# A 128-byte tile that nobody uses, placed ahead of the activation tiles in SBUF

## The chip, the cores and the metric

The kernel runs on one core of one Trainium2 chip. The metric is the device time of one execution in microseconds (us), taken as the median of several runs. All inputs start in HBM and the output ends there.

## The reference

The computation is a block-local attention followed by a feed-forward layer with a squared ReLU. Only what matters is shown:

```python
# q, k, v: (8, 8, 576, 64) float32; w_in: (512, 2048), w_out: (2048, 512) float64
q_c, k_c, v_c = (t.reshape(B, H, S // 64, 64, D) for t in (q, k, v))
scores = np.matmul(q_c, k_c.transpose(0, 1, 2, 4, 3)) / np.sqrt(D)
attn = softmax(scores)                       # over each chunk of 64 keys
x = np.matmul(attn, v_c)                     # back to (4608 tokens, 512)
h = x @ w_in
g = np.maximum(h, 0.0) ** 2
out = g @ w_out                              # (4608, 512) float32
```

## The kernel before

**Tiling.** The 4608 tokens are 36 "pairs" of two 64-token chunks, 128 tokens each, and the pairs are gathered into nine blocks of four (512 tokens). A block's attention output is kept transposed in SBUF as two tiles, `xh` (the value rounded to the matmul's reduced float type) and `xl` (the remainder), made by `x_of`; there are two buffers of each, and block b uses buffer b % 2. The hidden dimension of 2048 is cut into 16 slices of 128.

**Feed-forward.** For each block and slice a `Step` does twelve 128x512 products into `h` (`mm_in`, L514): the stationary operand is a 128x128 piece of the weights `wi`, the moving operand is 512 columns of `xh` or `xl`, and each of the four pieces of the contraction takes three products (high by high, high by low, low by high). ScalarE takes the ReLU of `h` into `g` (L525), VectorE, or ScalarE in the first two blocks, squares it (L529, L531), and the square is split into `gh` (ScalarE, L538) and `gl` (VectorE, L541). Two slices later twelve products go into the four accumulators `o` (`mm_out`, L551): here pieces of `gh` or `gl` are stationary and 512 columns of `wo` move. That is 9 x 16 x 24 = 3456 products in all. After a block's last slice the accumulators are copied to `ob` (L565) and stored.

**Attention.** The first eight pairs go through the class `Pair`, in the opening of the kernel and beside the conversion of the weights. The other 28 go through `Quad`: every so often three small groups of products (L321, L331, L291) are put between two products of the feed-forward.

**Weights.** They come as 64-bit floats. For each of 32 items a DMA brings the raw words, and ScalarE and VectorE turn them into high and low parts in seven steps (L147 to L186), with a working tile from the pool `wst`.

**Order of work.** A `Plan` lists all operations with assumed costs, and a small list scheduler writes out each engine's instructions in a fixed order. It looks at costs, dependences and ranks; addresses in SBUF are no part of it.

**Places in SBUF.** The pools are opened one after the other and lie in that order in each partition: `const` (identity, the raw and converted weights, and the leading pairs' q and k under the same tags), `att` (four small tiles of 32 bytes, L427 to L447 and their like in `Quad`), `xp` (`xh`, `xl`, and in the end the last block's output under the same tag), `gp` (`g`, `gh`, `gl`, `ob`), `raw` (q and k as loaded), `wst`, and then the pools `nat` or `late` of the attention. In the built program of before, `const` tiles of the weights begin at byte 17,056 of the partition, `att` at 148,128, the first `xh` at 148,256 and `g` at 181,024. Weight tiles are 4096 bytes apart, the buffers of x 8192, those of g 2048, so that all large tiles of `const` begin 160 bytes past a multiple of 256, and all large tiles behind `att` 32 bytes past one. Of the leading pairs' value tiles `vbd` (L475), the first two lie in `nat` and the next two in `const`.

Of the kernel before, what the change touches and what calls it, by code (L numbers as in the profile page):

```python
# [10 lines left out]
F32 = mybir.dt.float32  # L11
# [9 lines left out]
def kernel(  # L21
# [24 lines left out]
    P = 128  # L46
# [28 lines left out]
    att = ctx.enter_context(tc.tile_pool(name="att", bufs=1))  # L75
# [4 lines left out]
        x: ctx.enter_context(tc.tile_pool(name=f"ps_{x}", bufs=1, space=bass.MemoryType.PSUM))  # L80
        for x in ("o", "h", "at")
    }
    turn_at = itertools.count()

    both = psum["at"].tile([P, 2, DM], F32, name="both", tag="both")
# [931 lines left out]
```

## Time and profile before

| | |
|---|---|
| median of 3 runs | 911.04 us (909.97 to 911.22) |
| the profiled execution's own time | 911.28 us |
| its span, first to last instruction | 909.5 us |
| mean granted TensorE clock | 0.997 |
| instructions | 14995 |

The profile names engines PE (TensorE's matmuls), PEld (its weight loads, which overlap the matmuls), DVE (VectorE), ACT (ScalarE), POOL (GpSimd) and SP (SyncE, which issues most DMAs). A group of instructions is named by its line in the kernel and by out<-in with the program's tile names. A window's row gives, for each engine, the busy time in that stretch and in brackets the number of instructions. The chain of waits follows the work that ended last back from the last instruction; each of its pieces has a start, a length in us and a name, with the number of instructions in it. "Issue" there is time in which an engine waited for nothing that the profile shows.

### The profile page before, as it was taken

What the parts mean: (1) busy time and instruction counts of PE and PEld (TensorE: products, weight loads), DVE (VectorE), ACT (ScalarE), POOL (GpSimd) and SP (SyncE); (2) the same over time, 40 slices, a digit from 0 to 9 for tenths busy, and PEclk for the clock granted to TensorE, in tenths of its full rate; (3) what the DMA queues carried; (4) which work ended last, traced back from release to release, by engine and by line L of the source; (5) the groups of instructions that cost most, each with busy time, mean ns of one, the idle gap of its engine ahead of it and who ended that gap; (6) DMA issues with size and microseconds to landing.
All of it is one profiled execution on the core that took longest, in us unless ns stands there. A gap on an engine that the chain in (4) does not pass through costs nothing.

```text
span 909.5 us, 14995 instructions
## 1 busy us (share of the span) xinstructions
PE 897.6 (99%) x6046; PEld 724.9 (80%) x6046; DVE 427.1 (47%) x746; ACT 329.9 (36%) x565; POOL 6.1 (1%) x12
## 2 busy tenths in 40 slices
PE   8899999999999999999999999999999999999998
PEld 7677777888888888888888888888888888878886
DVE  5999992333444445444443343444444443223222
ACT  4798873334322223222322222223222322222221
POOL 2000000000000000000000000000000000000000
PEclk9999999999999999999999999999999999999999
DMA  9876533222222223111311131123222210001001
GB/s 196 261 210 177 168 65 97 36 48 46 70 48 36 35 35 83 32 33 31 79 33 32 33 81 29 33 35 81 36 36 36 51 42 1 1 1 47 1 1 46
DMA packets 193237, 55.52 MB, mean 61 GB/s; under 512 B 178192, under 2 KB 186640, under 8 KB 193168
## 3 DMA queue, kind: packets, MB, share of 16 engines
q1 hardware_dynamic: 190912, 53.91, 25.7%
q8 instruction: 47, 0.77, 0.4%
q10 hardware_dynamic: 2256, 0.66, 0.3%
q14 instruction: 22, 0.18, 0.1%
HBM read 45.09 MB, written 9.44 MB: 60 GB/s over the span
## 4 chain that ended last, share of the span: by engine, by line
PE 90%; DVE 5%; ACT 3%; issue 1%; POOL 0%; POOLq 0%; ACTq 0%; DVEq 0%
PE h L514 41%; PE o L551 41%; PE both L331 2%; PE both L291 1%; PE pt L321 1%; DVE gl L541 1%; PE both L741 1%; DVE wia L172 0%; ACT qbd L413 0%; DVE wi L186 0%; DVE wia L165 0%; DVE woa L165 0%; PE sc L425 0%; ACT wi L177 0%; DVE woa L172 0%
## 5 line engine op out<-in xcount | busy, mean ns | idle before, releaser
L514 PE MATMUL h<-xh,wi 128*128 128x512 f32 x1152 | 393.4, 398 | 0.1
L551 PE MATMUL o<-wo,gh 128*128 128x512 f32 x1152 | 361.7, 395 | 0.4 <-ACT ob L565 0.4
L514 PEld LDWEIGHTS h<-xh,wi 128*128 128x128 f32 x1152 | 216.1, 188 | 52.2 <-DVE wi L186 0.5
L551 PEld LDWEIGHTS o<-wo,gh 128*128 128x128 f32 x1152 | 215.8, 188 | 50.8 <-ACT ob L565 0.9
L551 PE MATMUL o<-wo,gl 128*128 128x512 f32 x576 | 227.0, 394 | 0.0
L514 PE MATMUL h<-xl,wi 128*128 128x512 f32 x576 | 226.0, 393 | 0.0
L541 DVE TENSOR_TENSOR gl<-g,gh 128x512 fp32r<-128x512 f32 x144 | 99.3, 690 | 207.3 <-ACT gh L538 204.2
L538 ACT CAST gh<-g 128x512 fp32r<-128x512 f32 x144 | 89.4, 621 | 225.7 <-PE o L551 188.4
L525 ACT ACTIVATE g<-h 128x512 f32<-128x512 f32 x144 | 85.6, 594 | 228.8 <-PE h L514 226.5
L529 DVE TENSOR_TENSOR g<-g 128x512 f32<-128x512 f32 x112 | 76.4, 682 | 184.9 <-ACT g L525 184.9
L551 PEld LDWEIGHTS o<-wo,gl 128*128 128x128 f32 x576 | 108.1, 188 | 25.7
L514 PEld LDWEIGHTS h<-xl,wi 128*128 128x128 f32 x576 | 108.5, 188 | 24.0
L297 DVE TENSOR_REDUCE m<-both 128x8 f32<-128x512 f32 x28 | 19.3, 691 | 55.9 <-ACT xh L341 51.8
L307 ACT ACTIVATE e<-e 128x512 f32<-128x512 f32 x28 | 17.7, 632 | 49.6 <-DVE e L301 49.6
L327 ACT COPY p<-pt 128x512 f32<-128x512 f32 x28 | 16.4, 585 | 20.4 <-PE pt L321 20.4
L341 ACT CAST xh<-both 128x512 fp32r<-128x512 f32 x28 | 16.4, 587 | 14.4 <-PE both L291 13.4
L531 ACT ACTIVATE g<-g 128x512 f32<-128x512 f32 x32 | 20.3, 635 | 0.6
L343 DVE TENSOR_TENSOR xl<-both,xh 128x512 fp32r<-128x512 f32 x28 | 19.1, 681 | 2.1 <-ACT xh L341 2.1
L277 DVE STREAM_TRANSPOSE qt<-q_raw 128x512 f32<-128x512 f32 x28 | 19.6, 700 | 0.0
L331 PEld LDWEIGHTS both<-p,v_raw 64*64 64x64 f32 x896 | 15.6, 134 | 4.9 <-issue 4.9
L331 PE MATMUL both<-p,v_raw 64*64 64x64 f32 x896 | 19.4, 224 | 0.0
L316 DVE TENSOR_TENSOR e<-e,z 128x512 f32<-128x512 f32 x28 | 19.2, 685 | 0.1
(85 smaller groups left out, 461.6 us busy)
## 6 DMA issues: line engine op xcount, KB each, us to landing
wiraw<-in_moe_w_in_dram SPq DMA_DIRECT2D x16, 512.0 KB, 6.6
woraw<-in_moe_w_out_dram SPq DMA_DIRECT2D x16, 512.0 KB, 5.8
out_dram<-ob SPq DMA_DIRECT2D x32, 256.0 KB, 2.0
q_raw<-in_q_dram SPq DMA_DIRECT2D x224, 32.0 KB, 2.2
k_raw<-in_k_dram SPq DMA_DIRECT2D x224, 32.0 KB, 2.2
v_raw<-in_v_dram SPq DMA_DIRECT2D x56, 128.0 KB, 3.3
vbd<-in_v_dram SPq DMA_DIRECT2D x32, 64.0 KB, 3.3
qk_raw<-in_q_dram SPq DMA_DIRECT2D x14, 128.0 KB, 4.8
```

The lines of the kernel that those rows point to most:

```text
L277: nc.vector.transpose(t.rearrange("p h i -> p (h i)"), pairs[self.pair][nm].rearrange("p h a d -> p (h a d)"))
L297: nc.vector.tensor_reduce(self.m, four[:, :, 0], axis=AX.X, op=ALU.max)
L316: nc.vector.tensor_tensor(self.e, self.e, self.z.broadcast_to([P, HH, 2, CH]), op=ALU.mult)
L331: nc.tensor.matmul(four[to, c, 1, h2], self.v[own, 2 * h2 + w], self.p[own, h2, w], start=True, stop=True)
L343: nc.vector.tensor_tensor(xl, four[:, :, 1], xh.bitcast(F32), op=ALU.subtract)
L514: nc.tensor.matmul(self.h[:, :self.n], a[:, c], bb[:, c, :self.n], start=c == 0 and i == 0, stop=last,)
L525: nc.scalar.activation(self.g, self.h[:, :self.n], AF.Relu)
L529: nc.vector.tensor_tensor(self.g, self.g, self.g, op=ALU.mult)
L531: nc.scalar.activation(self.g, self.g, AF.Square)
L538: nc.scalar.copy(self.gh[:, :self.n], self.g)
L541: nc.vector.tensor_tensor(self.gl[:, :self.n], self.g, self.gh.bitcast(F32)[:, :self.n], op=ALU.subtract)
L551: nc.tensor.matmul(acc[b, j], a[:, j * P:(j + 1) * P], bb, start=f == 0 and i == 0, stop=f == NF - 1 and i == 2,)
```

## The change

One tile of 128 partitions by 32 float32 values, 128 bytes in each partition, is taken from the pool `att` ahead of everything else in it. Nothing writes it and nothing reads it.

```diff
--- before.py
+++ after.py
@@ -80,6 +80,7 @@
         x: ctx.enter_context(tc.tile_pool(name=f"ps_{x}", bufs=1, space=bass.MemoryType.PSUM))
         for x in ("o", "h", "at")
     }
+    att.tile([P, 32], F32, name="edge")
     turn_at = itertools.count()
 
     both = psum["at"].tile([P, 2, DM], F32, name="both", tag="both")
```

The instructions of all five engines, and their order, are the same in both built programs (2757 rows of PE in the merged listing, 747 of DVE, 564 of ACT, 17 of POOL, 175 of SP). What differs is the place in SBUF of everything behind `const`: the small tiles of `att`, `xh`, `xl`, `g`, `gh`, `gl`, `ob`, `raw`, `wst`, `nat` and `late` all lie 128 bytes higher, the first `xh` at 148,384. The tiles of `const` and everything in PSUM stay where they were. The moved large tiles thus begin 160 bytes past a multiple of 256, as the weights do and did. The last tile ends 128 bytes later, at byte 228,256 of the partition.

## The prediction

> **What bounds the kernel now.** I read the page first, then the chain of waits, the windows by stage, and last the groups by line.
>
> ```profile
> span 909.5 us, 14995 instructions
> PE 897.6 (99%) x6046; PEld 724.9 (80%) x6046; DVE 427.1 (47%) x746; ACT 329.9 (36%) x565; POOL 6.1 (1%) x12
> PE 90%; DVE 5%; ACT 3%; issue 1%; POOL 0%; POOLq 0%; ACTq 0%; DVEq 0%
> ```
>
> PE is busy in 99% of the span, and it holds 90% of the chain that ended last. So TensorE sets the time in nine tenths of the chain; where the other tenth lies, the windows show (busy us, and instructions in brackets):
>
> ```profile
> core 0: us, PE busy (x) PEld busy (x) DVE busy (x) ACT busy (x) POOL busy (x), PEclk, DMA share, GB/s
> 0.00:33.00 33.00, 27.90 (x380) 23.44 (x381) 23.21 (x45) 17.90 (x32) 6.05 (x12) 0.95 0.93 230
> 33.00:117.00 84.00, 81.45 (x584) 63.43 (x582) 81.00 (x160) 73.21 (x133) 0.00 (x0) 1.00 0.67 192
> 230.00:806.00 576.00, 576.00 (x3935) 467.81 (x3936) 243.89 (x410) 165.17 (x277) 0.00 (x0) 1.00 0.20 41
> ```
>
> In the first 117 us VectorE is the full engine (81.00 of 84 us between 33 and 117): the weights are converted there and PE waits for it. From 230 to 806 us PE is never idle, and DVE and ACT work less than half the time. A change that adds no instruction can therefore act in three ways only: the pace of a product in the PE stage, the length of a vector or scalar instruction in the opening, or the landing of a transfer that somebody waits for. The pace comes from the chain, which merges the twelve products of a group (start us, length us):
>
> ```profile
> 521.23 2.78 PE o L551 x12
> 524.01 2.78 PE h L514 x12
> 537.93 2.78 PE o L551 x12
> 540.71 0.69 PE h L514 x3
> 810.55 2.80 PE h L514 x12
> 813.35 2.80 PE o L551 x12
> 897.25 8.42 PE o L551 x36
> ```
>
> From 521.23 to 540.71 there are seven groups in 19.48 us, 2.783 us each or 231.9 ns a product. From 810.55 to 897.25 there are 31 groups in 86.70 us, 2.797 us each or 233.1 ns a product. So there are two paces, 0.014 us a group apart, and each holds for long stretches with `h` and `o` alike; between them lies an insertion of attention products or a wait. I take the pace for a rhythm into which PE falls after a disturbance. What picks it the trace does not tell, and that matters for a rival below.
>
> **The change part by part.**
>
> *The tile itself.* It has no writer and no reader: no instruction, no wait, no transfer. The five instruction streams are the same in both programs, so no queue is passed and no wait is added. Cost: 0.
>
> *The products of the feed-forward.* In `h` a stationary weight piece (160 past a multiple of 256) meets a moving piece of x (now 32 past, then 160). In `o` it is the other way round: g is stationary and moved, `wo` moves through PE and keeps its place. If the distance between the two operands within 256 bytes set the pace, it would change from 128 to 0 for all 3456 products. The trace of before has one place where the same instruction stands at both distances: the values of the leading pairs, L475, where `vbd` of pairs 0 and 1 lies behind `att`, like the other operand `tt`, and that of pairs 2 and 3 in `const`. Pair 0, at distance 0, and pair 3, at distance 128:
>
> ```profile
> 17.99 1.15 PE L475 MATMUL both<-tt,vbd 128*64 128x64 f32 x32
> 31.34 1.15 PE L475 MATMUL xt<-tt,vbd 128*64 128x64 f32 x32
> ```
>
> Both take 1.15 us for 32. That is a narrower product (64 columns, not 512), so it bounds rather than proves: one step of the printed 0.01 us in 1.15 is 0.9%. The second bound is the pair of paces above. If all went at 2.783, the groups that ran at 2.797 would gain; if all went at 2.797, the long middle would lose. The counts per stretch, from the windows of L514 and of L551 in that order:
>
> ```profile
> 117.00:183.00 66.00, 32.78 (x134) 24.68 (x133) 1.00 0.28 58
> 196.00:230.00 34.00, 15.91 (x63) 11.74 (x63) 1.00 0.28 48
> 230.00:806.00 576.00, 289.85 (x1155) 215.18 (x1156) 1.00 0.20 41
> 806.00:906.00 100.00, 49.08 (x200) 37.12 (x198) 1.00 0.04 14
> ...
> 117.00:183.00 66.00, 33.34 (x132) 24.54 (x132) 1.00 0.28 58
> 196.00:230.00 34.00, 17.83 (x72) 13.44 (x72) 1.00 0.28 48
> 230.00:806.00 576.00, 282.72 (x1152) 216.63 (x1152) 1.00 0.20 41
> 806.00:906.00 100.00, 55.88 (x228) 42.79 (x228) 1.00 0.04 14
> ```
>
> Slow stretches: (134 + 132 + 63 + 72 + 200 + 228) / 12 = 69 groups, worth 69 x 0.014 = 1.0 us. Fast stretch: (1155 + 1152) / 12 = 192 groups, worth 192 x 0.014 = 2.7 us. So the term lies between -1.0 and +2.7 us. I take 0, since L475, the row where the distance alone differs, shows nothing.
>
> [...]
>
> *Vector and scalar instructions of the opening.* These are the instructions that fill 81.00 us of DVE between 33 and 117. Some mix a tile of `const` with a moved one, some use moved tiles alone:
>
> ```profile
> L541 DVE TENSOR_TENSOR gl<-g,gh 128x512 fp32r<-128x512 f32 x144 | 99.3, 690 | 207.3 <-ACT gh L538 204.2
> L529 DVE TENSOR_TENSOR g<-g 128x512 f32<-128x512 f32 x112 | 76.4, 682 | 184.9 <-ACT g L525 184.9
> L186 DVE TENSOR_TENSOR wi<-wia,wi 128x512 fp32r<-128x512 f32 x16 | 10.9, 684 | 1.2 <-ACT wi L177 1.0
> L165 DVE SCALAR_TENSOR_TENSOR wia<-wiraw,wia 128x512 uint32<-128x512 uint32 x16 | 10.9, 683 | 0.1
> L186 DVE TENSOR_TENSOR wo<-woa,wo 128x512 fp32r<-128x512 f32 x16 | 10.8, 676 | 0.4 <-ACT wo L177 0.4
> L538 ACT CAST gh<-g 128x512 fp32r<-128x512 f32 x144 | 89.4, 621 | 225.7 <-PE o L551 188.4 <-DVE g L529 37.3
> L177 ACT CAST wi<-wia 128x512 fp32r<-128x512 f32 x16 | 9.9, 619 | 4.9 <-DVE wia L172 4.8
> ```
>
> `gl` and the square read and write moved tiles alone (690 and 682 ns); L186 and L165 mix the two sides (676 to 684 ns). The casts of ScalarE are 621 ns within the moved tiles and 619 ns from a moved tile into `const`. Mixed or not, the vector rows lie between 676 and 690 ns, 1% to either side of their middle, and the larger value belongs to instructions that start after a wait. On 81.00 us of DVE, 1% is 0.8 us; so this term lies between -0.8 and +0.8 us, and I take 0.
>
> *Transfers.* What the opening waits for goes into `const` (the weights' words, and the leading pairs' q and k) and stays in place; of what it waits for only `vbd` of pairs 0 and 1 is moved. In the stretch from 230 to 806 us PE is never idle, so nothing that lands there is waited for. The end is the one place where a transfer from a moved tile is bare: the last half of the last store, issued by ACT.
>
> ```profile
> out_dram<-ob_last SPq DMA_DIRECT2D x1, 128.0 KB, 2.0
> out_dram<-ob_last ACTq DMA_DIRECT2D x1, 128.0 KB, 2.1
> ```
>
> The two halves of the last tile's store, equal in size, land in 2.0 and 2.1 us, so 0.1 us to either side is what I allow, and take 0. [...]
>
> **The sum.** Profiled execution 911.28 us (its span of 909.5 and 1.8 around it) + 0 + 0 + 0 + 0 = 911.28 us. The median of before is 0.24 us below its profiled execution, so in medians the forecast is **911.0 us**. The three runs of before spread from 909.97 to 911.22, that is 0.14%; a difference under 0.2% (1.8 us) is about what a measurement of this kernel cannot tell from none.
>
> **The rivals.**
>
> *Slower: the middle falls into the slow rhythm.* If the rhythm depends on where the operands lie, or on how the first products after an insertion meet, the 192 groups between 230 and 806 us may run at 2.797 us as the last 31 do. For it: both paces occur in one execution of one program, so something slight decides. Against: through that whole stretch every insertion was followed by the fast pace, and x alternates there between two buffers 16,384 bytes apart. Price 2.7 us, time 911.0 + 2.7 = 913.7 us. It counts as slower from 1.8 / 0.014 = 129 groups on, two thirds of the middle. Chance 0.12.
>
> *Faster: the distance of 128 costs something now.* If products slow down when their operands lie 128 apart within 256 bytes, the change takes the cost away in all 3456. For it: two paces exist, so a product of 512 columns can be quicker than another. Against: L475, and the vector rows, which make no difference between mixed and unmixed. Priced with the one step that the trace shows, 0.014 us in each of the 288 groups, it is 4.0 us, and the time 907.0 us; it counts as faster from 1.8 / 288 = 6 ns a group on, half a nanosecond a product. The slow stretches turning fast alone are 1.0 us and stay inside the band. Chance 0.08.
>
> *The change does not do what it says.* A tile without a reader could have been left out of the layout. But the built program has x at 148,384 and not 148,256, so it is moved; had it not been, the forecast would be the same 911.0 us. No chance of its own.
>
> **How the numbers follow.** The forecast, nothing that can be measured, has the remaining 0.80. The low end is the forecast with all slow groups turned fast and a run as far below its median as the lowest of before was: 911.04 - 0.97 - 1.07 = 909.0 us. That also holds the vector term's -0.8. The high end is the slower rival with a run as far above: 913.7 + 0.2 = 913.9 us. What is left out is the faster rival. Chances: faster by over 0.2% is 0.08, within 0.2% is 0.80, slower by over 0.2% is 0.12. The likeliest case by itself is 909.2 to 912.8 us.
>
> **What would show it.** In the profile after: groups of twelve at 2.783 us between 230 and 806 us and at 2.797 at the end; the vector rows between 676 and 690 ns; 81 us of DVE between 33 and 117; the last store in 2.0 to 2.1 us. If the middle shows 2.80, the slower rival is right. If a third pace appears, or L551 and L514 part from each other, the place of the operands matters in a way that L475 did not show. If the opening ends at another time than 117 us with the same paces behind it, the cause is in the vector stage or in a transfer.

## The result and the profile after

The changed kernel takes 895.03 us (894.47 to 895.51, 4 runs) against 911.04 us (909.97 to 911.22): a ratio of 0.9826, 95% interval 0.9809 to 0.9843. That is 16.0 us or 1.7% less, outside the range of 909.0 to 913.9 us and on the side to which the prediction gave 0.08. The span fell from 909.5 to 893.7 us, by 15.8 us.

The page of the changed kernel, for the rows that showed PE as the bound (every line of the kernel is one higher, so L514 is now L515 and L551 is L552):

```profile
span 893.7 us, 14995 instructions
PE 880.9 (99%) x6046; PEld 724.0 (81%) x6046; DVE 427.2 (48%) x746; ACT 330.6 (37%) x565; POOL 6.1 (1%) x12
```

The same instructions, and the loads, vector and scalar engines have the same busy time within 1 us; only PE is busy for 16.7 us less, in the same share of the span. So the products themselves follow each other faster. The windows by stage say where not to look, and where to look:

```profile
33.00:117.00 84.00, 80.60 (x584) 63.28 (x582) 81.11 (x160) 73.23 (x132) 0.00 (x0) 1.00 0.70 196
800.00:870.00 70.00, 70.00 (x311) 57.97 (x310) 19.29 (x28) 17.06 (x28) 0.00 (x0) 1.00 0.04 16
```

The opening does the same work in the same time (DVE 81.11 of 84 us, before 81.00). Near the end, where there is nothing but the feed-forward, 70 us hold 311 products. A stretch of the same length near the end of the kernel before holds 302, with PE just as full, the clock at 1.00 in both, and the vector and scalar engines as lightly loaded:

```profile
810.00:880.00 70.00, 70.00 (x302) 56.38 (x301) 18.68 (x27) 16.40 (x27) 0.00 (x0) 1.00 0.04 16
```

The chain of waits of the changed kernel gives the pace, in the middle and at the end (start us, length us):

```profile
511.28 2.28 PE h L515 x9
513.57 2.72 PE o L552 x12
516.29 2.72 PE h L515 x12
519.01 2.72 PE o L552 x12
...
532.61 0.68 PE h L515 x3
...
873.53 2.72 PE h L515 x12
881.70 8.17 PE o L552 x36
```

Seven groups of twelve from 513.57 to 532.61 take 19.04 us: 2.720 us each, 226.7 ns a product, and the end runs at the same pace. Before it was 2.783 in the middle and 2.797 at the end. This is the third pace that the prediction named as the sign that the place of the operands matters. `h` and `o` show it alike.

**The sum made again.** The 192 groups of the middle gain 0.063 us each, 12.1 us, and the 69 slow ones 0.077 us each, 5.3 us; together 17.4. What does not gain is the rest of a group behind an insertion of attention: its nine products took 2.28 us before and take 2.28 us now (first row above, and here before):

```profile
517.86 0.63 PE both L331 x32
518.48 0.47 PE both L291 x32
518.95 2.28 PE h L514 x9
```

With one insertion for each of the 28 later pairs that is some 28 x 9/12 x 0.063 = 1.3 us less, so 16.1 us, against 15.8 measured. Nothing else is needed to explain the time: the vector rows are where they were (690 and 682 ns for `gl` and the square, mean of one).

```profile
L542 DVE TENSOR_TENSOR gl<-g,gh 128x512 fp32r<-128x512 f32 x144 | 99.4, 690 | 199.9 <-ACT gh L539 196.7
L530 DVE TENSOR_TENSOR g<-g 128x512 f32<-128x512 f32 x112 | 76.4, 682 | 176.0 <-ACT g L526 176.0
```

So is the last store within 0.1 us (2.0 and 2.1 us before), in the view of DMA issues (KB each, us to landing):

```profile
out_dram<-ob_last SPq DMA_DIRECT2D x1, 128.0 KB, 2.0
out_dram<-ob_last ACTq DMA_DIRECT2D x1, 128.0 KB, 2.2
```

### The profile page after: what moved, and what is told of

It reads as the page before. It is cut to its first block, busy times and chain, and to the rows that moved or that the text cites. A ratio compares the mean times of both kernels' runs of the same rounds, so it can differ in the third digit from the quotient of the medians.

```text
span 893.7 us, 14995 instructions
## 1 busy us (share of the span) xinstructions
PE 880.9 (99%) x6046; PEld 724.0 (81%) x6046; DVE 427.2 (48%) x746; ACT 330.6 (37%) x565; POOL 6.1 (1%) x12
## 4 chain that ended last, share of the span: by engine, by line
PE 85%; DVE 5%; DMA 4%; ACT 3%; SPq 2%; issue 1%; DVEq 0%; ACTq 0%
PE h L515 40%; PE o L552 40%; PE both L332 2%; DMA wiraw<-in_moe_w_in_dram 2%; PE both L292 2%; PE pt L322 1%; SPq L250 1%; DMA qk_raw<-in_k_dram 1%; DMA k_raw<-in_k_dram 1%; DVE woa L166 0%; DVE gl L542 0%; SPq L133 0%; DVE wia L173 0%; DVE woa L173 0%; ACT qbd L414 0%
## 5 line engine op out<-in xcount | busy, mean ns | idle before, releaser
L515 PE MATMUL h<-xh,wi 128*128 128x512 f32 x1152 | 388.2, 394 | 0.2
L552 PE MATMUL o<-wo,gh 128*128 128x512 f32 x1152 | 356.1, 390 | 0.5 <-ACT ob L566 0.5
L515 PEld LDWEIGHTS h<-xh,wi 128*128 128x128 f32 x1152 | 216.0, 188 | 47.4 <-DVE wi L187 0.5
L552 PEld LDWEIGHTS o<-wo,gh 128*128 128x128 f32 x1152 | 215.3, 188 | 45.5 <-ACT ob L566 0.9
L552 PE MATMUL o<-wo,gl 128*128 128x512 f32 x576 | 224.3, 389 | 0.0
L515 PE MATMUL h<-xl,wi 128*128 128x512 f32 x576 | 223.8, 389 | 0.0
L552 PEld LDWEIGHTS o<-wo,gl 128*128 128x128 f32 x576 | 108.1, 188 | 22.8
L515 PEld LDWEIGHTS h<-xl,wi 128*128 128x128 f32 x576 | 108.2, 188 | 21.4
```

The costliest lines, as they stand in the source:

```text
L515: nc.tensor.matmul(self.h[:, :self.n], a[:, c], bb[:, c, :self.n], start=c == 0 and i == 0, stop=last,)
L552: nc.tensor.matmul(acc[b, j], a[:, j * P:(j + 1) * P], bb, start=f == 0 and i == 0, stop=f == NF - 1 and i == 2,)
```

## The experiments

**What has to agree: each tile with a fixed place, or the two operands with each other.** Three kernels put the 128 bytes elsewhere, and a fourth puts 256 in the place of the change. In all of them the instructions and their order are those of before.

*Everything moved, weights too* (`e1_all`):

```diff
+    const.tile([P, 32], F32, name="edge")      # ahead of the identity and the weights
```

> The 128 bytes stand ahead of the weights too, so that weights, x and g all lie 128 bytes higher and their distances are those of the kernel before. Distance theory (a product is slow when its two operands lie 128 apart within 256 bytes, quick when they agree): 911 us, groups of twelve at 2.78 to 2.80 us as before. Place theory (what counts is where x and g lie by themselves, 160 and not 32 past a multiple of 256): 895 us, groups at 2.72. Neighbour theory (the other moved tiles, those of the attention and the loads, set the rhythm): 895 us as well, since they are moved as in the change.

Measured: 910.71 us, ratio to before 0.9999 (0.9989 to 1.0008). In the chain the groups are those of before, although x and g lie exactly where the change puts them:

```profile
504.44 2.78 PE h L515 x12
507.22 2.78 PE o L552 x12
510.01 2.78 PE h L515 x12
```

So the place theory and the neighbour theory both fall: it is the distance to the weights that counts.

*Only g moved, and only x moved* (`e2_g`, `e3_x`):

```diff
 e2_g
+    gp.tile([P, 32], F32, name="edge", bufs=1)       # ahead of g
 e3_x
+    att.tile([P, 32], F32, name="edge")              # ahead of x
+    gp.tile([P, 32], F32, name="edge2", bufs=1)      # ahead of g: 256 in all
```

> The 128 bytes stand behind x and ahead of g: g and all behind it lie as in the change, x as before. Distance theory: the products with g (into o) at 2.72 us a group, those with x (into h) at 2.78, half of the 16 us: 903 us. Place theory: the same numbers. Neighbour theory: both at 2.72, 895 us. If the weight load alone decides (g is loaded, x moves through): o 2.72 and h 2.78 too, to be set against the next kernel.

> 128 bytes ahead of x and 128 more ahead of g: x lies as in the change, g and all behind it 256 bytes higher than before, so as before within 256. Distance theory and place theory: h at 2.72 us a group, o at 2.78, 903 us. Neighbour theory: 911 us, both at 2.78. If the load of g alone decides: 911 us; if it is the operand that moves through PE alone: 903 us with h quick here, and nothing gained with g moved alone.

Measured: 904.37 us with g alone, ratio 0.9931 (0.9915 to 0.9948); 908.33 us with x alone, ratio 0.9974 (0.9964 to 0.9985). Each time the line whose operands agree is the quick one. The chain with g alone:

```profile
501.66 2.79 PE h L515 x12
504.45 2.73 PE o L552 x12
507.19 2.79 PE h L515 x12
```

and with x alone:

```profile
522.14 2.76 PE h L516 x12
524.90 2.80 PE o L553 x12
527.70 2.76 PE h L516 x12
```

In `o` the moved tile is the loaded operand, in `h` the moving one, and either helps; so neither the load nor the moving stream alone decides. But the gains are 6.4 and 2.4 us, 8.8 together, where I expected two halves of 16; 908.33 us with x alone misses the 903 of every theory that had `h` quick. The starts of the products of one quick group each tell why, as distances from each to the next in ns (g alone, then x alone):

```
o, g alone:  232 233 230 227 227 226 227 227 226 227 227 226
h, x alone:  236 224 231 236 228 232 231 227 227 226 227 232
```

In these two, a quick group that follows a slow one needs three and seven products until it goes at 227. Where quick and slow groups alternate every twelve products, much of the gain is used up at the seams (the quick groups take 2.73 and 2.76 us, against 2.72 with both quick); with both quick there are no seams but those of the attention. The slow groups pay a little too: 2.79 and 2.80 us in the rows above, where before had 2.78.

*256 bytes* (`e4_256`):

```diff
+    att.tile([P, 64], F32, name="edge")
```

> 256 bytes ahead of x and g. If the period is 256 bytes (distance or place): 911 us, groups at 2.78 to 2.80. If it is 512 or more, or if it is the rhythm that falls anew with every layout: some other pace; at 2.72 the time is 895 us.

Measured: 910.71 us, ratio 0.9998 (0.9989 to 1.0007), with this in the chain:

```profile
505.09 2.78 PE h L515 x12
507.88 2.78 PE o L552 x12
510.66 2.78 PE h L515 x12
```

A distance of 128 bytes and one of 128 + 256 are alike here. The pace did not fall anew with this layout, nor with that of `e1_all` (2.78 us a group in both).

**How near is near enough.** Four sizes of the unused tile put x and g 64 and 32 bytes below the weights' offset within 256, and 32 and 64 above.

```diff
+    att.tile([P, N // 4], F32, name="edge")    # N = 64, 96, 160, 192
```

> The unused tile is 64 bytes: x and g begin 96 past a multiple of 256, the weights 160 past one, 64 bytes apart. Match theory (quick only where the two operands of a product agree within 256 bytes): 911 us, groups at 2.78 to 2.80. Half theory (quick where both begin in the same half of 128 bytes of the 256): x and g begin in the lower half and the weights in the upper, so 911 us. Graded theory (the farther apart, up to 128, the slower): halfway, 903 us, groups at 2.75.

> The unused tile is 96 bytes: x and g begin 128 past a multiple of 256, 32 bytes below the weights' 160. Match theory: 911 us, 2.78 to 2.80 a group. Half theory: both in the upper half, 895 us, 2.72. Graded theory: 899 us, 2.735.

> The unused tile is 160 bytes: x and g begin 192 past a multiple of 256, 32 bytes above the weights' 160. Match theory: 911 us, 2.78 to 2.80 a group. Half theory: both in the upper half, 895 us, 2.72. Graded theory: 899 us, 2.735, as with 32 bytes below.

> The unused tile is 192 bytes: x and g begin 224 past a multiple of 256, 64 bytes above the weights' 160. Match theory: 911 us, 2.78 to 2.80 a group. Half theory: both in the upper half, 895 us, 2.72. Graded theory: 903 us, 2.75, as with 64 bytes below.

One run each, beside 911.29 us for a run of before on the same chip: 911.00 (64), 914.00 (96), 913.84 (160), 910.98 us (192). The half theory and the graded theory both fall: next to agreement it is not quicker but slowest. The match theory stands in that nothing but agreement is quick, but it has no word for the 3 us by which 32 bytes are slower than 64 and 128. The chain at 32 bytes above (160) and at 64 above (192):

```profile
503.60 2.80 PE o L552 x12
506.40 2.80 PE h L515 x12
509.20 2.80 PE o L552 x12
```

```profile
501.86 2.80 PE o L552 x12
504.66 2.76 PE h L515 x12
507.43 2.80 PE o L552 x12
510.23 2.79 PE h L515 x12
```

At 64 bytes below (64) the two lines change places:

```profile
502.77 2.76 PE o L552 x12
505.53 2.80 PE h L515 x12
```

In both runs only the line whose moving operand begins 64 bytes above its loaded one, within 256, has groups of 2.76 us: from 230 to 895 us these are 32 of 88 whole groups of `h` in `s192` and 80 of 112 of `o` in `s64`. Its other groups, and all of the line that has it 64 below, take 2.79 to 2.80. So which of the two lies higher counts as well as the distance, though in the time far less than agreement does (910.98 and 911.00 us, where the change takes 895.03).

*Agreement elsewhere* (`both0`, `s384`):

```diff
 both0
+    const.tile([P, 24], F32, name="edge0")     # weights at a multiple of 256
+    att.tile([P, 32], F32, name="edge")        # x and g at a multiple of 256
 s384
+    att.tile([P, 96], F32, name="edge")
```

> 96 bytes ahead of the weights and 128 ahead of x: weights, x and g all begin exactly on a multiple of 256. Match theory (only the agreement of a product's two operands within 256 bytes counts): 895 us, groups at 2.72, as in the change. Boundary theory (a start on the multiple itself saves something more): below 893 us, groups under 2.72.

> 384 bytes ahead of x and g: they agree with the weights within 256 bytes as in the change, and now also within 512 (in the change they are 256 apart within 512). Period of 256: 895 us, 2.72 a group. Period of 512 with the best place at 256: 911 us or in between.

Measured: 894.97 us for `both0`, ratio 0.9825 (0.9811 to 0.9838), the same as the change; 895.53 us in one run for `s384`. The chain of `both0`, and then that of `s384`:

```profile
826.91 2.72 PE o L553 x12
829.63 2.72 PE h L516 x12
```

```profile
827.31 2.72 PE o L552 x12
830.03 2.72 PE h L515 x12
```

Between these layouts it made no difference where the agreeing operands begin (894.97 and 895.03 us), and agreement within 512 added nothing to agreement within 256 (895.53). No layout tried beats that of the change.

**What one product pays.** Two kernels start from the change and put only one of the low halves 128 bytes off.

```diff
 e6_gl: the change, and in Step.high between gh and gl, once
+    gp.tile([P, 32], F32, name="edge2", bufs=1)
 e7_xl: the change, and in x_of, for both buffers, ahead of xl and behind it
+    xp.tile([P, 32], F32, name=...)
```

> The change, and 128 bytes more between gh and gl, so that one of three products into o (gl as the loaded operand) has operands 128 apart and all others agree. Single-product theory (each product pays for its own pair): a third of what was lost where all of o was off, 4 us, 899 us; the products with gl are slow and the others at 227 ns. Settling theory (after an off product several more are slow until PE is back in step, as the six to eight slow ones at each start of a quick group suggest): near the loss of all of o, 13 us, 908 us, with no 227 ns left in o.

> The change, and 128 bytes more between xh and xl, so that one of three products into h (xl as the moving operand) has operands 128 apart and all others agree. Single-product theory: a third of what was lost where all of h was off, 3 us, 898 us. Settling theory: near the loss of all of h, 9 us, 904 us, with no 227 ns left in h.

One run each: 901.01 and 899.06 us. In the first the groups of `o` lengthen and those of `h` stay:

```profile
826.61 2.77 PE o L553 x12
829.38 2.72 PE h L515 x12
```

and in the second it is the other way round:

```profile
827.80 2.75 PE h L519 x12
830.55 2.72 PE o L556 x12
```

The distances from each start to the next in one such group, in ns:

```
o, gl off:  gh 227  gh 232  gl 234 | gh 227  gh 233  gl 234 | gh 226  gh 233  gl 234 | ...
h, xl off:  xh 226  xl 234  xh 226 | xh 227  xl 234  xh 226 | xh 227  xl 234  xh 226 | ...
```

The settling theory falls: 227 ns stand right beside 234, and the other line is untouched. The slow start of a whole quick group behind a whole slow one, seen with g or x alone, does not follow a single off product; what makes it is not shown. The instructions of VectorE and ScalarE are those of the change, and neighbours in time differ by 7 ns (227 beside 234), so their work does not explain the difference either.

The single-product theory gives the form, but not quite the size. With `xl` off, one product in three pays 7 ns, 3.5 us in the runs (899.06 against 895.53 for `s384` on the same chip; 3 expected). With `gl` off, the product with `gl` pays 7 and the one ahead of it 6: the groups of `o` are 0.05 us longer, 7 us over 144 groups, where 4 was expected. The single run is 5.5 us above `s384`, but its granted clock is 1.000 and that of `s384` 0.998; it is 7 us above the two runs of `both0` at 1.000 (893.86 and 894.05). The product ahead is the one during which the trace has the load of `gl`. So it looks as if a product pays both for the piece that it is multiplied with and for the piece that is being loaded meanwhile; but an after-effect of the load on the product behind it would leave the same pattern, and no run tells the two apart.

**Why the narrow product did not show it.** Two kernels cut each product into `h` into two of 256 columns:

```diff
-            nc.tensor.matmul(self.h[:, :self.n], a[:, c], bb[:, c, :self.n], ...)
+            for k in range(2):
+                r = slice(k * self.n // 2, (k + 1) * self.n // 2)
+                nc.tensor.matmul(self.h[:, r], a[:, c], bb[:, c, r], ...)
 e9_half_after also
+    att.tile([P, 32], F32, name="edge")
```

> Each product into h is cut into two of 256 columns with the same weights loaded twice; x and g lie as before, 128 from the weights. This run is the base for the next; o stays at 512 columns and at its slow pace, 2.76 to 2.80 us a group. The weight load's record is 188 ns long before, so a product of 256 columns cannot follow in half of 232 ns if loads set its pace: a group of h then takes up to 24 x 188 = 4.5 us instead of 2.8.

> The same with x and g as in the change. Stream theory (an off stream pays about 7 ns a product or 3% of its length, whatever its length): the groups of h are 0.06 to 0.15 us shorter than in the run before, and those of o 2.72 to 2.75. Hidden theory (where the weight load takes the time, the distance is covered by it): the groups of h are as long as in the run before within 0.01 us, and only o is shorter.

One run each: 918.11 us at the places of before, 916.03 at those of the change. The chain at the places of before, then at those of the change:

```profile
842.24 2.78 PE o L553 x12
845.02 2.85 PE h L516 x24
```

```profile
840.37 2.75 PE o L554 x12
843.12 2.87 PE h L517 x24
```

Both expectations miss, and so does the estimate of up to 4.5 us: a group of 24 half products takes only 2.85 us, 119 ns each, though the record of one weight load is 188 ns long in this run too (mean of the 3456 for `h`); so the records of successive loads overlap. With operands that agree, the half products are not quicker but a trace slower, 2.87 us, and only `o`, at 512 columns, gains. So the gain shows at 512 columns and is gone at 256, with the same operands and the same type. Whether the shorter stream has no such cost, or something else that sets the 119 ns covers it, these two runs do not tell. Either way L475, with 64 columns, was no test for products of 512.

## Why the prediction was wrong

**What was right.** PE bounds the kernel (busy in 99% of the span before and after), a tile that nobody uses costs nothing by itself (with the 256 bytes of `e4_256` the ratio is 0.9998), the order of instructions is untouched, and the vector instructions, the opening and the last store kept their durations. The list of the three ways in which the change could act was complete, and the one that acted was the first, the pace of a product.

**The step that failed.** It is the one on the products of the feed-forward, which put this term of the sum at nothing: "I take 0, since L475, the row where the distance alone differs, shows nothing". The runs showed 0.063 us in a group of the middle and 0.077 in one of the slow stretches, and 16.0 us in all. In the trace of the changed kernel pair 0 and pair 3 have equal operand distances, and both rows still read 1.15 us:

```profile
17.96 1.15 PE L476 MATMUL both<-tt,vbd 128*64 128x64 f32 x32
31.21 1.15 PE L476 MATMUL xt<-tt,vbd 128*64 128x64 f32 x32
```

The observation was sound, but it did not carry over. I had called it a bound, of 0.9%, and then used it across an eightfold difference in width. Nor did I keep to it: 0.9% of 288 groups of 2.783 us is 7 us, and the range allowed far less. The row differs in type as well: `tt` and `vbd` are plain float32, and each of the 16 instructions for a pair leaves two records, while x, g and the weights are of the reduced type, with one record for each product. Which of the two differences hid the effect at 64 columns is open; at 256 columns of the reduced type it has already gone (2.85 us a group of `h` apart, 2.87 in agreement).

**The second error is in the bounds.** I bounded the pace from both sides by the two paces that the trace of before shows, 2.783 and 2.797. Both belong to operands that disagree by 128: they are two rhythms of the same layout, and the pace of the other layout, 2.720, lies outside them. A bound may only be taken from rows in which the quantity that changes takes both values. No wide product of before was in agreement, so the low end of this term was unknown, and the range should have reached lower.

**The rivals.** The faster one had the right mechanism, operands 128 apart within 256 bytes, in all 3456 products, and a chance of 0.08. Its price was 0.014 us a group, 4.0 us, from that same pair of paces, a quarter of the 16.0 us that came. The slower one did not come: no group of the changed kernel's middle ran at 2.80.

**What stays open.** For this kernel the runs show the rule, agreement within 256 bytes (226.7 ns a product), and its price, 3 to 7 ns in a product of 512 columns by the distance (230 to 233 ns). They do not show what in the hardware makes it. Why 32 bytes off is a little slower than 128, why it counts at 64 which of the operands lies higher, and why the half products lose a trace with agreement, is not explained. The four sizes between, `s384`, the kernels with one low half off and those with half products were run once each.

## What to carry to other kernels

Where a kernel is bound by wide float32 products (here of the reduced type), compare where the loaded and the moving operand begin within 256 bytes, and try a pool padded so that they agree; here 128 unused bytes were worth 1.7% (895.03 against 911.04 us), and leaving them out loses as much unseen. The sign is in the trace: an even 226 or 227 ns from start to start in the changed kernel (all products between 800 and 880 us), against an uneven 228 to 241 in that of before (between 524 and 538 us), with a mean of 232. And a row shows that something costs nothing only for products of the same width and type as those in question.

## What the runs showed of the hardware that was not expected

- Here a 512-column product of the reduced type follows the last after 226.7 ns when its operands begin at the same place within 256 bytes, and after 230 to 233 ns at every other distance tried (32, 64 and 128 bytes to either side, in steady groups of one kind).
- It is the distance of the two operands and not the place of either: with all moved by the same 128 bytes the time was 910.71 us, as before (ratio 0.9999). At 64 bytes (`s64`, `s192`) there were groups of 2.76 us only with the moving operand above the loaded one; with it below all took 2.79 to 2.80.
- After a whole group that is off, an agreeing group took three products (g alone) and seven (x alone) to reach 227 ns in the two groups listed; that is much of why g alone and x alone brought 6.4 and 2.4 us where both brought 16.0.
- Half products of 256 columns followed each other every 119 ns (2.85 us for 24), so that cutting all of `h` in two cost only some 7 to 8 us in 911 at the places of before.
